# Transposing u with the DMA crossbar in an attention and mixer kernel, and splitting its last output chunk

## The chip, the core and the metric

The kernel runs on one core of a Trainium2 chip, as one launch. The metric is device time in microseconds (us), the median of several runs.

The core has a matrix engine (TensorE, PE in the profile; its weight loads are listed apart as PEld), a vector engine (VectorE, DVE), a scalar engine (ScalarE, ACT), GpSimd (POOL) and a sync engine (SyncE, SP) that here only issues DMAs. PE writes to PSUM; DVE and ACT move the results from there to SBUF, the on-chip memory from which PE reads.

## The reference

Blockwise causal attention over 8 batches, 8 heads, 576 positions and a head width of 64, and behind it one mixer layer with a token part and a channel part:

```python
# B, H, S, D = 8, 8, 576, 64; blocks of 64
scores = scale * np.matmul(q, k.transpose(0, 1, 3, 2))
scores = np.where(block_i >= block_j, scores, -1e9)
attn = softmax(scores)                      # with + 1e-09 in the denominator
x = (attn @ v).transpose(0, 2, 1, 3).reshape(B, S, 512)

xt = x.transpose(0, 2, 1)
h  = np.maximum(xt @ w_tok1, 0.0) @ w_tok2  # w_tok1 576 x 256, w_tok2 256 x 576
u  = x + h.transpose(0, 2, 1)
h2 = np.maximum(u @ w_ch1, 0.0) @ w_ch2     # w_ch1 512 x 1536, w_ch2 1536 x 512
out = u + h2                                # float32, 8 x 576 x 512
```

Inputs are float32; the kernel works in bfloat16 with float32 sums in PSUM.

## The kernel before

Each batch goes through these stages.

- **Attention** (scores at L415, exponentials on ACT at L444, product with v at L514, division on DVE at L535 and L541). It leaves x of the batch in `x_sb`, positions on the partitions, in five chunks of 128 positions (the last holds 64).
- **Token mix** (`token_mix`). Matmuls at L592 give `aT`; matmuls at L663 give h in the layout of x, and DVE adds x to it at L684. This leaves u in `u_sb`: four chunks of 128 positions by 512 channels. The last 64 positions of an even batch and of the odd batch behind it share one chunk, `um_sb`, one per pair of batches.
- **Transpose of u.** Channel-up needs u with the channels on the partitions. For batch 0 (`direct`), PE computes the transposed u by matmuls (L621, L636). For every later batch, PE transposes each 128×128 block of u against an identity matrix (L697), four blocks to one PSUM bank, and ACT or DVE copies the bank (L712, L714) to `uT`, or to `umT` for the shared chunk, which is transposed with the odd batch.
- **Channel-up** (`channel_up`): 12 column groups of 4 matmuls of 512 columns (L736), 48 matmuls a batch, then a ReLU on ACT or DVE to `gT` (L560, L562). The shared chunk does the same with 128 columns (`channel_up_mixed`, L763).
- **Channel-down** (`channel_down`): four chunks of 12 matmuls (L802), an add of u on DVE into `o_sb` (L818), and a store. Two chunks share one `o_sb` buffer and one store of 512 KB (L839). The shared chunk (`mixed=True`) has 12 matmuls, one add and two stores of 128 KB (L831), one to each batch of its pair. All stores go out on SP's queue.

Buffers come in rings: `uT` and `umT` have two, `u_sb`, `x_sb` and `o_sb` three, the PSUM pool `mm` four banks. `uT` of batch b is buffer b modulo 2, so it is free when the channel-up of batch b − 2 has read it. `o_sb` buffers are taken in turn by a counter, `out_n`, two for a batch and one for a shared chunk: the last store of batch 7 reads buffer 0, and the last shared chunk of all, the kernel's final work, gets buffer 1.

The order of instructions is not that of the program text. Every piece of work is an `Op` with engines it may run on, a cost, its dependences, a priority (lower goes first), and buffers that it takes and gives. `Plan.run` simulates the engines with these costs and lists the ops by planned start; the instructions are then issued in that order on each engine's queue, and each queue runs in order. Waits for real dependences are put in by the framework. A DMA has a cost on its issuing queue and a transfer time `xfer`, behind which its users become ready. Attention has priorities around −1000, token mix around −500, the channel stages from 0 up, so channel work fills the time that attention and token mix leave on PE. After attention ends, only channel work and the last token mixes are left.

L318 and L296 are the q and k loads and their transposes on DVE, L343 the v loads, all issued from POOL.

Of the kernel before, what the change touches and what calls it, by code (L numbers as in the profile page):

```python
# [11 lines left out]
BF16 = mybir.dt.bfloat16  # L12
# [3 lines left out]
ADD = mybir.AluOpType.add  # L16
# [113 lines left out]
def kernel(  # L130
# [26 lines left out]
    def ring(n, shape, dtype, name, pool=sb):  # L157
        return [pool.tile(shape, dtype, name=f"{name}{i}", uniquify=False) for i in range(n)]
# [10 lines left out]
    x_sb = ring(3, [128, 5, DM], BF16, "x_sb")  # L169
    u_sb = ring(3, [128, 4, DM], BF16, "u_sb")  # L170
    um_sb = ring(2, [128, DM], BF16, "um_sb")
    uT = ring(2, [128, NDM, 512], BF16, "uT")
    umT = ring(2, [128, NDM, 128], BF16, "umT")
    aT = ring(2, [128, NDT, DM], BF16, "aT")
    gT = ring(2, [128, NDC, 512], BF16, "gT")
# [25 lines left out]
    def bank_of(note):  # L201
        return mm[note["slot"]]
# [4 lines left out]
    def reads(key, op):  # L207
        readers.setdefault(key, []).append(op)
        return op

    def reuse(key):
        return readers.pop(key, [])

    def mm_cost(n, count):
        return count * max(n / 2400 + 0.003, 0.033)
# [4 lines left out]
    def dve_cost(n, speed=1):  # L220
        return 0.09 + n * 0.00104 / speed
# [343 lines left out]
    def token_mix(b, x_done, w1_ready, w2_ready):  # L565
# [14 lines left out]
        for half in range(NH):  # L580
            cols = slice(W * half, W * half + W)
            xs = x_done[8 // NH * half : 8 // NH * (half + 1)]
            p0 = prio + ((-494, -600)[half] if direct else 0)
            a_done = []
            for tts in ((0, 1),) if direct else ((0,), (1,)):
                bank = {}

                def emit(o, tts=tts, bank=bank, cols=cols):
                    for n, tt in enumerate(tts):
                        for c in range(5):  # L590
                            w = w1o_sb if c == 4 and odd else w1_sb[:, c]
                            nc.tensor.matmul(  # L592
                                out=bank_of(bank)[:, W * n : W * n + W],
                                lhsT=w[:, 128 * tt : 128 * (tt + 1)],
                                rhs=xt[:, c, cols],
                                start=(c == 0),
                                stop=(c == 4),
                            )

                op = P.add(  # L600
                    "PE", mm_cost(W, 5 * NH), emit, xs + w1_ready[odd] + a_war, p0,
                    take=[(BANK, bank)], urgent=direct and half == 1,
                )
                reads(("x", b % 3), op)

                def emit(o, tts=tts, bank=bank, cols=cols):
                    relu(
                        o,
                        at[:, tts[0] : tts[-1] + 1, cols],
                        bank_of(bank).rearrange("p (t d) -> p t d", d=W),  # L610
                    )

                a_done.append(P.add(EVAC, evac_cost(512), emit, [op], p0, give=[bank], urgent=direct and half == 1))
            a_all += a_done
            for m in range(NDM // NH * half, NDM // NH * (half + 1)) if direct else ():
                bank = {}

                def emit(o, m=m, bank=bank):
                    ps = bank_of(bank)
                    for c in range(4):  # L620
                        nc.tensor.matmul(  # L621
                            out=ps[:, 128 * c : 128 * c + 128],
                            lhsT=xt[:, c, 128 * m : 128 * (m + 1)],
                            rhs=ident,
                            start=(c == 0),
                            stop=False,
                        )

                first = P.add(
                    "PE", mm_cost(128, 4), emit, xs + pads["ident"] + uT_war, p0 + 1,  # L630
                    take=[(BANK, bank)], urgent=half == 1,
                )

                def emit(o, m=m, bank=bank):
                    for t in range(NDT):
                        nc.tensor.matmul(  # L636
                            out=bank_of(bank),
                            lhsT=at[:, t, 128 * m : 128 * (m + 1)],
                            rhs=w2_sb[:, t, 0:512],
                            start=False,  # L640
                            stop=(t == NDT - 1),
                        )

                op = P.add("PE", mm_cost(512, 2), emit, a_done + w2_ready + [first], p0 + 1, urgent=half == 1)
                reads(("a", b % 2), op)
                reads(("x", b % 3), op)

                def emit(o, m=m, bank=bank):
                    if o.engine == "ACT":
                        nc.scalar.copy(uT[b % 2][:, m, :], bank_of(bank))  # L650
                    else:
                        nc.vector.tensor_copy(uT[b % 2][:, m, :], bank_of(bank))

                done.append(P.add(EVAC, evac_cost(512), emit, [op], p0, give=[bank], urgent=direct and half == 1))
        if direct:
# [31 lines left out]
            reads(("x", b % 3), op)  # L687
            u_done.append(op)

        for si in range(4 * direct, 4 + odd):  # L690
            bank = {}

            def emit(o, si=si, bank=bank):
                ps = bank_of(bank).bitcast(BF16)[:, 0:512]
                src = ut[:, si, :] if si < 4 else umt
                for m in range(NDM):
                    nc.tensor.transpose(  # L697
                        ps[:, 128 * m : 128 * (m + 1)], src[:, 128 * m : 128 * (m + 1)], ident
                    )

            deps = [u_done[si]] + pads["ident"]
            deps += uT_war if si < 4 else reuse(("umT", pair % 2)) + um_first[pair]
            op = P.add(
                "PE", mm_cost(128, 4), emit, deps, prio + 2 + 0.1 * si, take=[(BANK, bank)]
            )
            reads(("u", b % 3) if si < 4 else ("um", pair % 2), op)

            def emit(o, si=si, bank=bank):
                ps = bank_of(bank).bitcast(BF16)[:, 0:512].rearrange("p (m s) -> p m s", m=NDM)
                dst = uT[b % 2][:, :, 128 * si : 128 * si + 128] if si < 4 else umT[pair % 2]  # L710
                if o.engine == "ACT":
                    nc.scalar.copy(dst, ps)  # L712
                else:
                    nc.vector.tensor_copy(dst, ps)  # L714

            op = P.add(
                EVAC, {"ACT": act_cost(512), "DVE": dve_cost(512, 2)}, emit, [op], prio, give=[bank]
            )
            (done if si < 4 else um_done).append(op)
# [8 lines left out]
    def channel_up(b, uT_done, wc1_ready, prio):  # L728
        g_war = reuse(("g", b % 2))
        done = []  # L730
        for cc in range(NDC):
            bank = {}

            def emit(o, cc=cc, bank=bank):
                for m in range(NDM):
                    nc.tensor.matmul(  # L736
                        out=bank_of(bank),
                        lhsT=wc1_sb[:, m, 128 * cc : 128 * (cc + 1)],
                        rhs=uT[b % 2][:, m, :],
                        start=(m == 0),  # L740
                        stop=(m == NDM - 1),
                    )

            op = P.add("PE", mm_cost(512, 4), emit, uT_done + wc1_ready[cc] + g_war, prio + 0.1 * cc, take=[(BANK, bank)])
            reads(("uT", b % 2), op)

            def emit(o, cc=cc, bank=bank):
                relu(o, gT[b % 2][:, cc, :], bank_of(bank))

            done.append(P.add(EVAC, evac_cost(512), emit, [op], prio, give=[bank]))  # L750
        return done
# [31 lines left out]

    out_n = [0]

    def channel_down(b, g_done, wc2_ready, u_done, prio, mixed=False):
        chunks = [None] if mixed else list(range(4))
        gt = gmT[b // 2 % 2] if mixed else gT[b % 2]
        ut = um_sb[b // 2 % 2] if mixed else u_sb[b % 3]
        for n, si in enumerate(chunks):  # L790
            bank = {}
            prev = None
# [6 lines left out]
            for part in range(3):  # L799
                def emit(o, part=part, c0=c0, bank=bank):  # L800
                    for cc in range(4 * part, 4 * part + 4):
                        nc.tensor.matmul(  # L802
                            out=bank_of(bank),
                            lhsT=gt[:, cc, c0 : c0 + 128],
                            rhs=wc2_sb[:, cc, :],
                            start=(cc == 0),
                            stop=(cc == NDC - 1),
                        )
# [98 lines left out]
```

## Time and profile before

| | |
|---|---|
| median of 3 runs | 330.89 us (330.43 to 331.6) |
| the profiled execution: its time | 328.57 us |
| the profiled execution: its span, first to last instruction | 326.8 us |
| mean granted PE clock | 0.977 |
| busy PE, DVE, ACT, POOL | 95%, 50%, 51%, 19% of the span |
| DMA, mean | 89 GB/s |

A row of the profile names the line of the kernel, the engine, the operation, what it writes and reads, shapes, a count (x), the busy time in us and the mean length of one in ns, and, behind the bar, how long the engine sat idle just before and what released it. A matmul's length is a latency in a pipeline, so matmuls overlap. A row of a table by stretches gives start and end, the length, then for each engine the busy time and the number of instructions, then the granted clock (1.00 is full), the DMA engines' share and GB/s. A row of the timeline gives start, length, engine, line and work.

### The profile page before, as it was taken

Reading aid. Unit: us, or ns where it says so; the run is one execution under the profiler, and the core shown is the slowest. Engines: PE = TensorE matmul, PEld = TensorE weight load, DVE = VectorE, ACT = ScalarE, POOL = GpSimd, SP = SyncE. Lnnn points to the kernel's source line nnn. Section 1 sums busy time; section 2 is a strip of 40 time slices with the busy share of each in tenths; the row PEclk is TensorE's granted clock in tenths of the full one; section 3 lists DMA queues with packets and bytes.
Section 4 is the critical chain, followed back from the end, with each engine's and each line's share of the span. In section 5 each row is a group of like instructions: output and inputs, shape, how many; then the busy total and the mean of one; then the engine's idle time right before and its main releaser. Section 6 shows DMA issues by size and latency. Waiting matters only on the chain.

```text
span 326.8 us, 7206 instructions
## 1 busy us (share of the span) xinstructions
PE 309.6 (95%) x3031; PEld 161.0 (49%) x3074; DVE 164.8 (50%) x383; ACT 167.6 (51%) x231; POOL 61.3 (19%) x97
## 2 busy tenths in 40 slices
PE   6799997999999999999999999999999999999994
PEld 2256454354556455454555456544544654444641
DVE  6637946696779498496574556035114112011012
ACT  4854873548769636648756766402702711613600
POOL 8657532411421502500500000000000000000000
PEclk9659999999999999999999999999999999999999
DMA  8999999957893907940901100013011002103013
GB/s 220 209 208 190 199 193 124 156 120 118 126 149 58 129 4 143 185 55 2 69 6 66 66 2 2 0 64 98 0 61 70 0 20 111 33 2 128 2 64 96
DMA packets 46800, 29.01 MB, mean 89 GB/s; under 512 B 34064, under 2 KB 37520, under 8 KB 46768
## 3 DMA queue, kind: packets, MB, share of 16 engines
q0 software_dynamic: 41200, 17.93, 44.9%
q1 hardware_dynamic: 5280, 10.03, 8.8%
q10 hardware_dynamic: 288, 0.59, 0.5%
q8 instruction: 24, 0.39, 0.5%
q14 instruction: 8, 0.07, 0.1%
HBM read 35.85 MB, written 9.44 MB: 139 GB/s over the span
## 4 chain that ended last, share of the span: by engine, by line
PE 85%; DVE 7%; ACT 3%; issue 2%; DMA 2%; ACTq 0%
PE mm L802 28%; PE mm L736 26%; PE sc L415 9%; PE mm L514 7%; PE mm L592 6%; PE mm L663 4%; PE mm L763 3%; DVE x_sb L541 2%; ACT e_sb L444 2%; DMA gT<-in_q_dram 2%; PE mm L697 1%; DVE u_sb L684 1%; DVE qT L318 1%; DVE rinv L535 1%; PE mm L636 1%
## 5 line engine op out<-in xcount | busy, mean ns | idle before, releaser
L444 ACT ACTIVATE e_sb<-sc 128x1024 bf16<-128x1024 f32 x96 | 93.2, 1021 | 49.0 <-PE sc L415 48.3
L736 PE MATMUL mm<-uT,wc_sb 128*128 128x512 bf16 x371 | 87.9, 379 | 1.1 <-issue 0.3
L802 PE MATMUL mm<-wc_sb,gT 128*128 128x512 bf16 x367 | 85.8, 379 | 1.3 <-issue 0.5
L560 ACT ACTIVATE gT<-mm 128x512 bf16<-128x512 f32 x73 | 43.5, 598 | 71.9 <-PE mm L736 71.6
L736 PEld LDWEIGHTS <-wc_sb 128*128 128x128 bf16 x384 | 36.2, 98 | 45.8 <-issue 4.5
L818 DVE TENSOR_TENSOR o_sb<-mm,u_sb 128x512 f32<-128x512 f32 x32 | 22.1, 691 | 70.9 <-PE mm L802 70.8
L802 PEld LDWEIGHTS <-gT 128*128 128x128 bf16 x384 | 36.1, 98 | 43.8 <-issue 3.9
L415 PE MATMUL sc<-qT,kT 32*128 32x64 bf16 (+4 forms) x768 | 39.2, 290 | 4.2 <-ACT e_sb L444 2.3
L343 POOL DMA_DIRECT2D v<-in_v_dram x35 | 29.6, 858 | 42.9 <-PE sc L415 21.0
L514 PEld LDWEIGHTS <-e_sb 128*128 128x128 bf16 x896 | 32.3, 99 | 10.1 <-issue 3.5
L514 PE MATMUL mm<-v,e_sb 128*128 128x65 bf16 x896 | 34.4, 196 | 2.0 <-DVE e_sb L486 1.9
L541 DVE TENSOR_TENSOR x_sb<-mm,rinv 128x320 bf16<-128x320 f32 x64 | 30.7, 488 | 1.6
L684 DVE TENSOR_TENSOR u_sb<-mm,x_sb 128x512 bf16<-128x512 f32 x32 | 20.9, 683 | 12.0 <-PE mm L663 11.8
L415 PEld LDWEIGHTS <-kT 32*128 32x128 bf16 x768 | 13.6, 95 | 25.1 <-issue 20.1
L562 DVE TENSOR_SCALAR gT<-mm 128x512 bf16<-128x512 f32 x23 | 15.8, 687 | 16.2 <-PE mm L736 16.1
L318 DVE STREAM_TRANSPOSE kT<-kraw 128x576 int32<-128x576 int32 (+1 forms) x20 | 20.1, 1029 | 1.6 <-PE sc L415 1.5
L318 DVE STREAM_TRANSPOSE qT<-qraw 128x576 int32<-128x576 int32 (+1 forms) x20 | 20.0, 1022 | 0.2
L663 PE MATMUL mm<-aT,w_sb 128*128 128x512 bf16 x72 | 19.7, 380 | 0.4 <-issue 0.2
L592 PE MATMUL mm<-x_sb,w_sb 128*128 128x512 bf16 (+1 forms) x81 | 18.1, 360 | 0.5 <-DVE x_sb L541 0.4
L486 DVE MEMSET e_sb<- 64x128 uint32 (+1 forms) x72 | 10.5, 153 | 15.3 <-ACT e_sb L444 12.2
L535 DVE RECIPROCAL rinv<-mm 128x5 f32<-128x5 f32 x64 | 11.2, 183 | 8.4 <-PE mm L514 8.1
L296 POOL DMA_DIRECT2D kraw<-in_k_dram x15 | 8.4, 559 | 27.9 <-DVE kT L318 13.9
(59 smaller groups left out, 188.2 us busy)
## 6 DMA issues: line engine op xcount, KB each, us to landing
out_dram<-o_sb SPq DMA_DIRECT2D x16, 512.0 KB, 2.8
kraw<-in_k_dram POOLq DMA_DIRECT2D x15, 288.0 KB, 5.7
qraw<-in_q_dram POOLq DMA_DIRECT2D x15, 288.0 KB, 6.5
v<-in_v_dram POOLq DMA_DIRECT2D x28, 128.0 KB, 5.7
wc_sb<-in_moe_w_ch_dram POOLq DMA_DIRECT2D x8, 192.0 KB, 8.4
wc_sb<-in_moe_w_ch_dram POOLq DMA_DIRECT2D x3, 512.0 KB, 10.1
gT<-in_v_dram POOLq DMA_DIRECT2D x4, 256.0 KB, 8.5
out_dram<-o_sb SPq DMA_DIRECT2D x8, 128.0 KB, 2.4
```

Source lines behind the costliest of these rows:

```text
L318: nc.vector.transpose(dst[:, 0:S, :] .rearrange("p s e -> p (s e)") .bitcast(I32) .rearrange("p (a k) -> p k a", k=NB)[:, k0:k1], raw2.bit ...
L343: nc.gpsimd.dma_start(out=dst, in_=src)
L415: nc.tensor.matmul(out=sc[h // 2][:, h % 2, c0 : c0 + w], lhsT=kT[i][r, j0 : j0 + 128, par], rhs=qT[i][r, i0 : i0 + w, par], start=(par == 0),
L444: nc.scalar.activation(dst, sc[h0 // 2][:, :, 0:n], EXP, scale=scale)
L514: nc.tensor.matmul(out=u[:, I, 0:65], lhsT=w, rhs=vt[:, J, head, 0:65], start=(J == 0), stop=(J == I),)
L541: nc.vector.tensor_tensor(out=xt[:, :, 64 * head : 64 * head + 64], in0=u[:, :, 0:64], in1=ri.to_broadcast([128, 5, 64]), op=MULT,)
L560: nc.scalar.activation(dst, src, RELU)
L592: nc.tensor.matmul(out=bank_of(bank)[:, W * n : W * n + W], lhsT=w[:, 128 * tt : 128 * (tt + 1)], rhs=xt[:, c, cols], start=(c == 0), stop ...
L663: nc.tensor.matmul(out=bank_of(bank), lhsT=w2_sb[:, t, c0 : c0 + 128], rhs=at[:, t, :], start=(t == 0), stop=(t == NDT - 1),)
L684: nc.vector.tensor_tensor(out=dst, in0=bank_of(bank)[r, :], in1=xt[r, si, :], op=ADD)
L736: nc.tensor.matmul(out=bank_of(bank), lhsT=wc1_sb[:, m, 128 * cc : 128 * (cc + 1)], rhs=uT[b % 2][:, m, :], start=(m == 0), stop=(m == NDM ...
L802: nc.tensor.matmul(out=bank_of(bank), lhsT=gt[:, cc, c0 : c0 + 128], rhs=wc2_sb[:, cc, :], start=(cc == 0), stop=(cc == NDC - 1),)
```

## The change

From batch 2 on, u is transposed by DMAs on SP's queue (`dma_start_transpose`) in place of PE's transposes and their copies. A batch has two of them, each for two chunks of 128 positions (128 × 1024 elements, 256 KB), with planned costs of 2.0 us on SP and 3.0 us of transfer; an odd batch has one more for the shared chunk (128 × 512, 128 KB). Batch 0 stays as it was, and batch 1 still transposes on PE, its shared chunk with it. `uT` is laid out as four position chunks of four channel groups of 128, in place of four channel groups of 512 positions, so channel-up's moving operand is now four runs of 128 columns.

The last shared chunk of the kernel is computed by `last_down`: two halves of 256 columns, each with 12 matmuls, an add of its own, and two stores of 64 KB, one issued from SP and one from ACT. The halves use `o_sb[0]` and `o_sb[1]`, and the plan lets a half's matmuls begin when the last store from its buffer is done.

```diff
-    uT = ring(2, [128, NDM, 512], BF16, "uT")
+    uT = ring(2, [128, 4, NDM, 128], BF16, "uT")
...
+                    ps = bank_of(bank).rearrange("p (c s) -> p c s", c=4)
                     if o.engine == "ACT":
-                        nc.scalar.copy(uT[b % 2][:, m, :], bank_of(bank))
+                        nc.scalar.copy(uT[b % 2][:, :, m, :], ps)
                     else:
-                        nc.vector.tensor_copy(uT[b % 2][:, m, :], bank_of(bank))
+                        nc.vector.tensor_copy(uT[b % 2][:, :, m, :], ps)
...
-        for si in range(4 * direct, 4 + odd):
+
+        crossbar = b >= 2
+        for f in range(2 if crossbar else 0):
+            def emit(o, f=f):
+                nc.sync.dma_start_transpose(
+                    out=uT[b % 2][:, 2 * f : 2 * f + 2].rearrange("p c m s -> p (c m) s"),
+                    in_=ut[:, 2 * f : 2 * f + 2, :].rearrange("p c d -> p (c d)"),
+                )
+
+            op = P.add("SP", 2.0, emit, u_done[2 * f : 2 * f + 2] + uT_war, prio, xfer=3.0)
+            reads(("u", b % 3), op)
+            done.append(op)
+        if crossbar and odd:
+            def emit(o):
+                nc.sync.dma_start_transpose(out=umT[pair % 2], in_=umt)
+
+            op = P.add("SP", 1.0, emit, [u_done[4]] + reuse(("umT", pair % 2)) + um_first[pair], prio, xfer=1.0)
+            reads(("um", pair % 2), op)
+            um_done.append(op)
+        for si in () if crossbar else range(4 * direct, 4 + odd):
...
-                dst = uT[b % 2][:, :, 128 * si : 128 * si + 128] if si < 4 else umT[pair % 2]
+                dst = uT[b % 2][:, si] if si < 4 else umT[pair % 2]
...
-                        rhs=uT[b % 2][:, m, :],
+                        rhs=uT[b % 2][:, :, m, :],
...
+    def last_down(gt, ut, deps, prio):
+        for f in range(2):
+            cols = slice(256 * f, 256 * f + 256)
+            bank = {}
+
+            def emit(o, cols=cols, bank=bank):
+                for cc in range(NDC):
+                    nc.tensor.matmul(
+                        out=bank_of(bank)[:, 0:256],
+                        lhsT=gt[:, cc, :],
+                        rhs=wc2_sb[:, cc, cols],
+                        start=(cc == 0),
+                        stop=(cc == NDC - 1),
+                    )
+
+            op = P.add("PE", mm_cost(256, NDC), emit, deps + reuse(("o", f)), prio + 0.1 * f, take=[(BANK, bank)])
+
+            def emit(o, f=f, cols=cols, bank=bank):
+                nc.vector.tensor_tensor(
+                    out=o_sb[f][:, 0, 0:256], in0=bank_of(bank)[:, 0:256], in1=ut[:, cols], op=ADD
+                )
+
+            op = P.add("DVE", dve_cost(256), emit, [op], prio, give=[bank])
+            for kk in range(2):
+                def emit(o, f=f, kk=kk, cols=cols):
+                    queue = nc.sync if o.engine == "SP" else nc.scalar
+                    queue.dma_start(
+                        out=out[B - 2 + kk, 512:576, cols],
+                        in_=o_sb[f][64 * kk : 64 * kk + 64, 0, 0:256],
+                    )
+
+                P.add(("SP", "ACT")[kk], 0.5, emit, [op], prio, xfer=4 * 0.06)
+
     def channel_down(b, g_done, wc2_ready, u_done, prio, mixed=False):
...
+        if mixed and b == B - 1:
+            return last_down(gt, ut, g_done + wc2_ready + u_done, prio)
```

## The prediction

> **What bounds the kernel now.** I read the page's busy times and slices first, then the chain that ended last, then busy time by stage.
>
> ```profile
> span 326.8 us, 7206 instructions
> PE 309.6 (95%) x3031; PEld 161.0 (49%) x3074; DVE 164.8 (50%) x383; ACT 167.6 (51%) x231; POOL 61.3 (19%) x97
> PEclk9659999999999999999999999999999999999999
> PE 85%; DVE 7%; ACT 3%; issue 2%; DMA 2%; ACTq 0%
> ```
>
> TensorE (PE) is busy 95% of the span, at the full granted clock after the first few slices, and carries 85% of the chain that ended last. Less PE work should shorten the span nearly one for one. The average hides stages, so I cut the span: attention with channel work as filler (57 to 209 us), then channel work alone (209 to 306).
>
> ```profile
> 57.00:134.00 77.00, 74.79 (x961) 40.11 (x974) 59.87 (x131) 50.15 (x64) 22.44 (x34) 1.00 0.86 114
> 134.00:209.00 75.00, 73.17 (x911) 39.99 (x922) 44.30 (x108) 48.64 (x67) 6.30 (x8) 1.00 0.33 42
> 209.00:306.00 97.00, 96.38 (x502) 46.42 (x511) 21.00 (x33) 32.31 (x55) 0.00 (x0) 1.00 0.14 49
> ```
>
> The columns are the stretch, then busy PE, weight loads, DVE, ACT, POOL, clock, DMA share, GB/s. PE idles 77 − 74.79 = 2.2, 75 − 73.17 = 1.8 and 0.6 us. It ends every stage last; DVE at 59.87 of 77 us is the only near rival, and only in the first.
>
> **What is removed: 108 transposes on PE.** The trace has 128 at L697 (112 of u_sb, 16 of um_sb). Batch 1 keeps 20; batches 2 to 7 lose 6 × 16 + 3 × 4 = 108. With them go their 27 copies out of PSUM.
>
> ```profile
> L697 PE MATMUL mm<-ident,u_sb 128*128 128x128 bf16 x112 | 9.1, 219 | 1.2 <-DVE um_sb L684 0.5 <-DVE x_sb L541 0.2
> L697 PE MATMUL mm<-ident,um_sb 128*128 128x128 bf16 x16 | 1.5, 218 | 0.1
> L712 ACT COPY uT<-mm 128x512 bf16<-128x512 bf16 x12 | 6.9, 595 | 1.5 <-PE mm L697 1.4
> L714 DVE COPY uT<-mm 128x512 bf16<-128x512 bf16 x16 | 6.2, 416 | 14.7 <-PE mm L697 14.5
> ```
>
> The 219 ns of one is a pipelined latency, not its price. The price is the time from the first transpose of a group to the start of PE's next work, read in the timeline of PE (start, length, work), one group per fence here:
>
> ```profile
> 98.14 1.13 PE L697 MATMUL mm<-ident,u_sb 128*128 128x128 bf16 x12
> 99.47 0.38 PE L697 MATMUL mm<-ident,u_sb 128*128 128x128 bf16 x4 [0.21 <-DVE um_sb L684]
> 99.80 0.59 PE L736 MATMUL mm<-uT,wc_sb 128*128 128x512 bf16 x2
> ```
> ```profile
> 235.69 1.29 PE L697 MATMUL mm<-ident,u_sb 128*128 128x128 bf16 x16
> 236.82 1.46 PE L802 MATMUL mm<-wc_sb,gT 128*128 128x512 bf16 x6
> ```
> ```profile
> 259.29 1.23 PE L697 MATMUL mm<-ident,u_sb 128*128 128x128 bf16 x16
> 260.36 1.95 PE L763 MATMUL mm<-umT,wc_sb 128*128 128x128 bf16 x32
> ```
>
> Late groups cost 236.82 − 235.69 = 1.13 and 260.36 − 259.29 = 1.07 us for 16, so 0.069 us each. The group at 98 us cost 99.80 − 98.14 = 1.66, since it waited for u to be added on DVE. Lower end: 108 × 0.069 = 7.4 us. Upper end: busy time of L697 alone over the seven stretches (each a group or two) that hold the 108, first and last stretch and the sum:
>
> ```profile
> 97.00:100.00 3.00, 1.39 (x16) 0.97 (x16) 1.00 0.33 57
> ...
> 259.00:260.60 1.60, 1.22 (x16) 0.97 (x16) 1.00 0.00 0
> sum 16.10, PE 8.67 PEld 6.80; mean PE 1.24 PEld 0.97
> ```
>
> 8.67 us counts each group's pipeline tail, which overlaps the next work, but leaves out its waits. I take 7.4: the waits for DVE stood in the attention stage, where PE may meet another wait in their place. The 27 copies (0.416 us on DVE, 0.595 on ACT) I cost at nothing: neither engine ends a stage. Where ACT and DVE are full, their absence helps a little.
>
> **What is added: 15 crossbar DMAs on SP's queue**, two of 256 KB for each of batches 2 to 7, one of 128 KB for each of batches 3, 5 and 7. Before, uT was ready a copy after the transposes; now after a DMA. What hides this is distance. uT has two buffers, so batch b's transpose can start when its u is added and the channel-up of batch b − 2 is done. The stretches below are cut at the channel-ups (busy time of L736 alone; the second bracket, weight loads, has x48 for a whole batch):
>
> ```profile
> 102.00:143.50 41.50, 0.36 (x2) 0.01 (x1) 1.00 0.87 107
> 143.50:161.60 18.10, 10.82 (x46) 4.28 (x48) 1.00 0.32 30
> 161.60:185.80 24.20, 0.30 (x2) 0.00 (x0) 1.00 0.31 57
> 185.80:200.30 14.50, 10.52 (x45) 4.37 (x48) 1.00 0.00 1
> 200.30:219.70 19.40, 0.42 (x2) 0.00 (x0) 1.00 0.07 28
> 219.70:234.60 14.90, 10.57 (x46) 4.66 (x48) 1.00 0.18 54
> 234.60:258.20 23.60, 10.66 (x49) 4.70 (x48) 1.00 0.12 45
> 258.20:273.10 14.90, 0.36 (x2) 0.00 (x0) 1.00 0.10 36
> 273.10:285.25 12.15, 10.42 (x47) 4.68 (x49) 1.00 0.22 65
> ```
>
> Batches 2 to 6 run their up in the stretches with x48 (x49 for the last), and batch 7 from 285.25. Batch 2's u is complete by 99.47, so 143.5 − 99.5 = 44 us. For the others I count from the buffer's release: batch 4 from 161.6 to 219.7, 58; batch 5 from 200.3 to 234.6, 34; batch 6 from 234.6 to 273.1, 38; batch 7 from 258.2 to 285.25, 27 us. The least is 27 for two DMAs in one queue: 13.5 us each.
>
> No row shows a crossbar transpose. Nearest rows, with KB each and us from issue to landing, and the software queue:
>
> ```profile
> out_dram<-o_sb SPq DMA_DIRECT2D x16, 512.0 KB, 2.8
> kraw<-in_k_dram POOLq DMA_DIRECT2D x15, 288.0 KB, 5.7
> out_dram<-o_sb SPq DMA_DIRECT2D x8, 128.0 KB, 2.4
> q0 software_dynamic: 41200, 17.93, 44.9%
> ```
>
> Lower end 2.4 us. Upper end from that queue's packets: 0.449 × 16 × 326.8 us / 41,200 = 57 ns of one engine for a packet. As 256-byte runs, 256 KB is 1,024 packets, so 57 ns × 1,024 / 16 = 3.6 us over 16 engines, about 6 with the 2.4 us. As 32-byte runs it is 29 us, beyond the cover. I take 6, which is nearest the 288 KB load's 5.7. Two cost 12 us, under 27: hidden, zero on the path. SP's queue is in order: a transpose behind a store whose data is late would wait with it, and a store behind a transpose would too. The planner orders SP by planned time, and stores fall inside channel-downs, after the release points above; I cost this at zero.
>
> The Trainium skill, "VectorE: DVE Perf Modes", The three transpose paths, speaks against the change: 390 ns for 128×128 on TensorE against 1309 ns through the crossbar, with the advice to use TensorE where PSUM will do. An estimate from that page: 8 blocks in series are 10.5 us, 21 for a batch, still under the 27, so by it the sum stands, but with only 6 us to spare. The trace's 0.069 us in a group already differs from its 390 ns; no run yet shows the 1309.
>
> **Layout.** uT becomes four 128-column pieces, so channel-up streams four runs. Its price if each run cost a separate 128-column matmul: 16 at 258.40 to 259.29 are 0.0556 each, four 0.2225, against 7.99 / 37 = 0.216 for 512 columns.
>
> ```profile
> 258.40 1.06 PE L763 MATMUL mm<-umT,wc_sb 128*128 128x128 bf16 x16
> 297.71 7.99 PE mm L736 x37
> ```
>
> So 0 to 384 × 0.0065 = 2.5 us; I take 0, since the instruction count and columns are the same. Copies into four runs exist before (L712, 595 ns) and cost no surcharge I can see.
>
> **The tail.** Before, the last chunk's add is followed by two stores from o_sb[1]: the buffers are taken in turn, modulo three. The new function names o_sb[0] and o_sb[1]; o_sb[0] is what batch 7's last store is still reading.
>
> ```profile
> 322.01 0.69 DVE L818 TENSOR_TENSOR o_sb<-mm,um_sb 128x512 f32<-128x512 f32 x1 [1.84 <-PE mm L802]
> ```
> ```profile
> 320.20 0.37 SPq L839 DMA_DIRECT2D out_dram<-o_sb  x1
> 322.73 1.11 SPq L831 DMA_DIRECT2D out_dram<-o_sb  x2
> ```
>
> Before: the second store starts at about 323.3 and lands 2.4 later, 325.7. After, in the same clock: the half in o_sb[0] must wait for the store issued at 320.20 to land, 320.20 + 2.8 = 323.0. Its add is some 0.4 us (an estimate, a little over half of 0.69), its stores go out at 323.4 on two queues and land at 325.8 or so: +0.1. The other half, planned first since its buffer is free, is done by then. Without that wait the add would start at 322.0 and all would end near 324.9, −0.8. Upper end +0.6, a second issue (1.11 / 2) in series. I take +0.1.
>
> **Sum.** −7.4 + 0 + 0 + 0.1 = −7.3. The profiled execution took 328.57 us around its span of 326.8, so 321.3 for it; the median of the runs shown is 330.89, so 323.6.
>
> **The rivals.**
> *The attention stage gives nothing back.* If ACT or DVE is what PE really follows there, only the transposes after 209 us count: 4 + 16 + 16 = 36, 36 × 0.069 = 2.5 us, so 328.4. For it: DVE's 59.87 of 77 us, and the wait at 99.47. Against it: PE idles only 2.2 and 1.8 us there, and channel work can always be drawn forward. 0.14.
>
> *The transposes are late (slower).* If one 256 KB DMA takes over 13.5 us, batch 7's channel-up waits for it. At 20 us: batch 7 stalls 40 − 27 = 13, batch 6 40 − 38 = 2, batch 5 (with its 128 KB) 50 − 34 = 16: 31 us, less 7.3, so some 355. The stalls of batches 7 and 5 together are 4.5 × D − 61, so the sign turns at D = 15 us. For it: no row shows such a DMA, and 32-byte runs would mean 29 us. Against it: 2.8 us for 512 KB. 0.09.
>
> *A new order eats it.* Every instruction after batch 2 is replanned. Doubling PE's 4.0 us of idle in 57 to 209, with the 2.5 us of the layout, leaves about 330.0. Nothing in the profile speaks for it. 0.09, of which 0.04 slower.
>
> **How the numbers follow.** My forecast has 0.68, its own range 321.4 (−8.67 and −0.8) to 326.2 (the layout's 2.5 us lost). Up to the attention rival gives 329.0; down, 321.0. What is left out, late transposes and a lost gain, is under 0.2. About 0.3%, 1.0 us, is what this measurement can tell from no change: faster 0.82, within 0.05, slower 0.13.
>
> **What the next profile would show.** Right: L697 with 20 matmuls, PE busy down by some 7 us, the 15 transposes at SP landing within about 6 us, no PE wait on a DMA before L736, L736 still at 0.216 us a matmul, and the first of the two last adds released by PE, the second by a DMA. Wrong: PE idle before L736 with a DMA as releaser, landings over 13 us, 4-run matmuls spaced wider, or PE idle in 57 to 209 above 4 us.

## The result, and the profile after

The changed kernel took 321.09 us (median; 319.41 to 321.27), against 331.25 us for the kernel before on the same chip. The ratio is 0.9685, with a 95% interval of 0.9646 to 0.9724: some 9 to 12 us faster. The forecast was 323.6 us, a gain of 7.3, in a range of 321.0 to 329.0. Scaled to the 330.89 of the forecast, the ratio makes 320.5, below the range. The direction held, and PE is what bounds the kernel, as forecast. The gain was some 3 us larger: about 2 us of that are in the work itself, about 1 in how runs of this kernel scatter (below).

The page of the changed kernel, its opening and the chain by engine:

```profile
span 319.2 us, 7057 instructions
PE 306.0 (96%) x2978; PEld 156.4 (49%) x2978; DVE 159.7 (50%) x370; ACT 160.7 (50%) x218; POOL 61.3 (19%) x97
PE 90%; ACT 3%; DMA 3%; DVE 2%; issue 1%; ACTq 0%; DVEq 0%
```

PE still bounds it, more clearly than before: 90% of the chain against 85%, and DVE's share fell from 7% to 2%. Weight loads fell from 3074 to 2978: 108 transposes gone, 12 matmuls more in the split tail. The same stretches as before show where PE idles now (0.5, 0.2 and 0 us):

```profile
57.00:134.00 77.00, 76.49 (x958) 39.46 (x956) 59.38 (x129) 48.31 (x61) 23.88 (x36) 1.00 1.02 135
134.00:209.00 75.00, 74.81 (x901) 38.77 (x900) 43.48 (x107) 46.22 (x61) 6.55 (x8) 1.00 0.43 52
209.00:306.00 97.00, 97.00 (x522) 46.93 (x521) 18.33 (x28) 32.24 (x54) 0.00 (x0) 1.00 0.24 62
```

These idle times mislead a little: the trace of before has 371 of 384 matmuls of L736, that of after all 384, and a missing record reads as idle. Start times of weight loads don't have that fault (x384 for L736), so from here I compare one stretch of equal work: from the middle of the first channel-down (its 25th matmul) to the start of the last channel-down. Cutting the executions there gives these rows, first of before, then of after (columns as in the tables by stretches):

```profile
68.15:308.83 240.68, 236.49 (x2329) 124.43 (x2362) 116.89 (x258) 126.33 (x180) 24.86 (x35) 1.00 0.37 61
```
```profile
69.85:300.88 231.03, 230.76 (x2256) 117.19 (x2254) 111.30 (x244) 119.44 (x167) 24.85 (x35) 1.00 0.51 79
```

The same work takes 9.65 us less at a clock of 1.00 in both. What lies ahead of it takes 69.85 − 68.15 = 1.7 us more in this execution of the changed kernel, which is clock (below), and the tail behind it 18.3 − 18.0 = 0.3 us more; both take away from the 9.65. A stretch cut like this repeats closely: 231.03 in a second profile of the same kernel, where the runs scatter over 2 us and more. It is the measure of the experiments.

The crossbar DMAs, from the rows of L695 (uT), and the tail on DVE:

```profile
L695 SPq DMA_TRANSPOSE uT<-u_sb x12: 1233/1254/1962, 97.1 to 253.1; - x12
DMA to landing us min/median/max: 3.3/4.5/5.9
```
```profile
311.54 0.69 DVE L873 TENSOR_TENSOR o_sb<-mm,u_sb 128x512 f32<-128x512 f32 x1 [0.17 <-PE mm L857]
312.80 0.42 DVE L824 TENSOR_TENSOR o_sb<-mm,um_sb 128x256 f32<-128x256 f32 x1 [0.56 <-PE mm L813]
315.25 0.42 DVE L824 TENSOR_TENSOR o_sb<-mm,um_sb 128x256 f32<-128x256 f32 x1 [2.04 <-DMA out_dram<-o_sb]
```

A 256 KB transpose lands 4.5 us after its issue, and no matmul waits for one. The second of the two last adds waits 2.04 us for the DMA that still reads o_sb[0].

### The profile page after: what moved, and what is told of

Read it like the earlier page. It is cut to its first block, busy times and chain, and to the rows that moved or that the text cites. A ratio compares the mean times of both kernels' runs of the same rounds, so it can differ in the third digit from the quotient of the medians.

```text
span 319.2 us, 7057 instructions
## 1 busy us (share of the span) xinstructions
PE 306.0 (96%) x2978; PEld 156.4 (49%) x2978; DVE 159.7 (50%) x370; ACT 160.7 (50%) x218; POOL 61.3 (19%) x97
## 3 DMA queue, kind: packets, MB, share of 16 engines
q1 hardware_dynamic: 19584, 13.44, 18.2%
## 4 chain that ended last, share of the span: by engine, by line
PE 90%; ACT 3%; DMA 3%; DVE 2%; issue 1%; ACTq 0%; DVEq 0%
PE mm L857 28%; PE mm L756 27%; PE sc L415 10%; PE mm L514 10%; PE mm L592 6%; PE mm L664 6%; PE mm L783 3%; ACT e_sb L444 2%; DMA gT<-in_q_dram 2%; DMA out_dram<-o_sb 1%; DVE qT L318 1%; PE mm L636 1%; DVE x_sb L541 0%; DVE o_sb L873 0%; DVE gT L562 0%
## 5 line engine op out<-in xcount | busy, mean ns | idle before, releaser
L857 PE MATMUL mm<-wc_sb,gT 128*128 128x512 bf16 x384 | 88.2, 379 | 0.0
L560 ACT ACTIVATE gT<-mm 128x512 bf16<-128x512 f32 x75 | 44.7, 598 | 69.8 <-PE mm L756 69.6
L514 PEld LDWEIGHTS <-e_sb 128*128 128x128 bf16 x896 | 33.4, 101 | 10.6 <-issue 4.1
L514 PE MATMUL mm<-v,e_sb 128*128 128x65 bf16 x896 | 35.4, 199 | 1.9 <-DVE e_sb L486 1.9
L541 DVE TENSOR_TENSOR x_sb<-mm,rinv 128x320 bf16<-128x320 f32 x64 | 30.9, 489 | 1.6
L562 DVE TENSOR_SCALAR gT<-mm 128x512 bf16<-128x512 f32 x21 | 14.4, 688 | 14.1 <-PE mm L756 14.1
L664 PE MATMUL mm<-aT,w_sb 128*128 128x512 bf16 x80 | 20.9, 380 | 0.0
L486 DVE MEMSET e_sb<- 64x128 uint32 (+1 forms) x72 | 10.5, 153 | 13.6 <-ACT e_sb L444 10.2
```

Source lines behind the costliest of these rows:

```text
L514: nc.tensor.matmul(out=u[:, I, 0:65], lhsT=w, rhs=vt[:, J, head, 0:65], start=(J == 0), stop=(J == I),)
L541: nc.vector.tensor_tensor(out=xt[:, :, 64 * head : 64 * head + 64], in0=u[:, :, 0:64], in1=ri.to_broadcast([128, 5, 64]), op=MULT,)
L560: nc.scalar.activation(dst, src, RELU)
L664: nc.tensor.matmul(out=bank_of(bank), lhsT=w2_sb[:, t, c0 : c0 + 128], rhs=at[:, t, :], start=(t == 0), stop=(t == NDT - 1),)
L857: nc.tensor.matmul(out=bank_of(bank), lhsT=gt[:, cc, c0 : c0 + 128], rhs=wc2_sb[:, cc, :], start=(cc == 0), stop=(cc == NDC - 1),)
```

## The experiments

Theories: **A**, the removed transposes were worth more than 7.4 us; **B**, the sum was right and the rest of the difference is the scatter of runs. When A held, it split: PE's waits for u, the copies, or a new order. "Stretch" is the one defined above.

**The changed kernel again.** No edit.

> The changed kernel again, beside the kernel before, so that each run's span and clock can be set side by side. Theory A (the removed transposes were worth more than priced: their whole stretches on PE, some 9 us, waits included): the ratio stays near 0.969, and the profile's stretch between the first channel-down and the last one is some 9.6 us shorter than before, 254.2 to about 244.6. Theory B (the sum of 7.3 was right and the rest of the measured 10 us is the clock: the profile shown of before missed a clock dip near 53 us that its other runs have): runs of before spread over 2 to 3 us with their granted clock, 0.977 for the short ones and 0.973 for the long ones, and runs of equal clock differ by 7.3 us only. Both can hold in part.

319.5 us, ratio 0.9693 (0.9647 to 0.9739). Both hold in part. The runs of before fall on steps with their granted clock: 328.8 us at 0.977, 330.2 to 331.1 at 0.970 to 0.971, 331.5 to 331.8 at 0.966 to 0.967. The changed kernel has 319.2 to 319.6 at 0.975 and longer ones at less. The forecast was drawn from an execution on the shortest step (328.57 at 0.977); like against like, 328.57 and 319.43 (this run's profiled execution), the gain is 9.1 us, not 7.3. So A carries the 2 us, and the uneven mix of steps the last one of the medians' 10.

**Crossbar without the split tail, and split tail without crossbar.**

```diff
-        if mixed and b == B - 1:
-            return last_down(gt, ut, g_done + wc2_ready + u_done, prio)
```

> The changed kernel with its last chunk computed and stored whole, as before: the crossbar and the layout alone. If the split tail costs 0.1 to 0.35 us, as its wait for the store of o_sb[0] suggests (add released by a DMA, 2.0 us of wait in the changed kernel's profile), this is 0.1 to 0.35 us faster than the changed kernel. Rival: the split gains the 0.8 us of an unhindered half, and this is some 0.8 us slower than the changed kernel.

> The kernel before with the split last chunk alone. Same question from the other side: between +0.35 and 0 us against before if the wait for o_sb[0] eats the split's gain, -0.8 us if it does not. In the profile one of the two 256-column adds is released by a DMA.

Crossbar alone: 321.35 us, ratio 0.9718 (0.9679 to 0.9757), stretch 231.03, tail 18.5. Split tail alone: 331.29, ratio 0.9996 (0.9969 to 1.0024), tail 18.2; its second add too was released by the out_dram DMA, after 2.05 us. All of the gain is the crossbar's. The split is worth nothing within 0.3 us; the tails of like kernels differ by 0.4 (18.3 and 18.7 of the same code), so its sign can't be told. The rival's −0.8 didn't come.

**Halves in free buffers.** The changed kernel with:

```diff
-    deps + reuse(("o", f))
+    deps + reuse(("o", f + 1))
...
-    out=o_sb[f][:, 0, 0:256]
+    out=o_sb[f + 1][:, 0, 0:256]
...
-    in_=o_sb[f][64 * kk : 64 * kk + 64, 0, 0:256]
+    in_=o_sb[f + 1][64 * kk : 64 * kk + 64, 0, 0:256]
```

> The changed kernel with the two halves in o_sb[1] and o_sb[2], whose stores are done or nearly done by then, in place of o_sb[0] and o_sb[1]. If the wait for the buffer is what ate the split's gain, the second add starts 0.1 us after its matmuls, some 1 us earlier than now, and the kernel is 0.8 to 1.1 us faster than the changed one. Rival (the stores themselves are the tail's bound, issue and landing in series): no change.

320.02 us, ratio 0.9676 (0.9642 to 0.971). The tail is 17.1 us against 18.3, and the second add is released by PE:

```profile
312.86 0.42 DVE L824 TENSOR_TENSOR o_sb<-mm,um_sb 128x256 f32<-128x256 f32 x1 [0.56 <-PE mm L813]
314.17 0.42 DVE L824 TENSOR_TENSOR o_sb<-mm,um_sb 128x256 f32<-128x256 f32 x1 [0.89 <-PE mm L813]
```

The buffer choice ate 1.2 us of the split. In medians the step is inside the scatter.

**The layout alone.** The changed kernel without the split tail and with all transposes back on PE; only `uT` in four pieces is left of the change.

```diff
-        crossbar = b >= 2
+        crossbar = b >= 99
```

> The kernel before with the new layout of uT alone (four runs of 128 columns for channel-up), transposes still on PE, last chunk whole. The prediction took 0 with an upper end of 2.5 us: 0 if the four runs stream as one, +2.5 us (channel-up matmuls spaced 0.2225 in place of 0.216 us) at the upper end. A gain would mean that the copies into the contiguous pieces are faster.

Ratio 0.9973 (0.9952 to 0.9995), and a stretch of 240.72 against 240.68: four runs of 128 columns cost nothing.

**The transposes back on PE, without the crossbar's being undone.** The changed kernel plus 27 groups of four transposes, of zeros. They have the old cost and priority but need no `uT` buffer, and the planner places them anew:

```diff
+            op = P.add(
+                "PE", mm_cost(128, 4), emit, [u_mm[si]] + pads["ident"] + pads["zeros"], prio + 2 + 0.1 * si,
+                take=[(BANK, bank)], give=[bank],
+            )
```

and the same of u, with `u_done[si]` as its dependence. Neither has copies.

> The changed kernel with 108 transposes put back on PE at the places of the old ones, but of a tile of zeros that is ready from the start, into a bank that nobody copies out. It gives back the slots on PE without the wait for u and without the copies. If only the slots count (108 x 0.069), it is 7.4 us slower than the changed kernel. If what was under-priced is the wait of PE for the DVE adds of u, some 2 to 2.5 us of the gain stay.

> As the run with zeros, but the 108 transposes read u, and so wait for the DVE add of their chunk, as they did before; still no copies. If PE's wait for u is the part that was under-priced, this is about 9 us slower than the changed kernel, 1.5 to 2 us slower than the run with zeros. If the 27 copies on ACT and DVE were the part, it is 7.4 us slower, as the run with zeros.

328.99 us (ratio 0.9923, 0.9901 to 0.9945) and 329.26 (0.9942, 0.9916 to 0.9969). The stretches, zeros first:

```profile
70.58:308.80 238.22, 235.28 (x2338) 124.08 (x2362) 107.35 (x238) 123.24 (x173) 24.91 (x35) 1.00 0.47 77
```
```profile
70.37:308.21 237.84, 234.77 (x2336) 123.88 (x2362) 108.03 (x239) 122.55 (x172) 24.86 (x35) 1.00 0.47 77
```

Against 231.03 that is +7.2 and +6.8 us. Placed as they are here, the transposes cost about what the slots were priced at, 7.4, and those of u no more than those of zeros. Some 2.5 to 2.8 us of the 9.65 are still missing. It doesn't follow that PE's wait for u cost nothing in the kernel before, because the order there was another; the orders are compared below.

**The copies back.** First beside the transposes of u, into a spare tile; then alone, from a ready tile in SBUF, so that no PSUM bank is held.

```diff
+            def emit(o, si=si, bank=bank):
+                ps = bank_of(bank).bitcast(BF16)[:, 0:512]
+                cast(o, spare[0 if o.engine == "ACT" else 1], ps)
+
+            P.add(EVAC, {"ACT": act_cost(512), "DVE": dve_cost(512, 2)}, emit, [op], prio, give=[bank])
```

> As the run whose 108 transposes on PE read u, with the 27 copies put back as well, on ACT or DVE as the planner has it, into a spare tile that nobody reads. Only the feeding of channel-up by the crossbar is left of the change. That run's stretch from the first to the last channel-down was 251.7 us, before it was 254.2, after 244.5. Theory C (the copies are the term priced wrong: costed at nothing, worth some 2 us): the stretch is 254 us or nearly so. Theory D (the copies are free as the prediction had it, and the 2 us are the luck of a new order): it stays near 251.7, within 0.7 us.

> The changed kernel with 27 copies of the old size alone on ACT or DVE, from a ready tile in SBUF (float32) into a spare tile, each behind the add of its chunk of u; no transposes on PE. If the copies cost by the time that they take from ACT and DVE, the stretch from the first to the last channel-down grows from 244.5 by 1.5 to 2.5 us. If they cost only by holding a PSUM bank and PE's hand-over, or not at all, it grows by less than 0.7 us.

With transposes and copies 332.48 us (ratio 1.0046, 1.0025 to 1.0066), copies alone 321.89 (0.9718, 0.9686 to 0.975):

```profile
71.20:312.22 241.02, 239.06 (x2364) 124.13 (x2362) 114.50 (x255) 128.27 (x183) 24.85 (x35) 1.00 0.46 76
```
```profile
71.50:302.55 231.05, 230.79 (x2256) 117.26 (x2254) 115.54 (x253) 128.90 (x185) 24.85 (x35) 1.00 0.51 79
```

Together all of the gain is gone (241.02 against 240.68 before). Alone they cost nothing (231.05), though DVE and ACT do 4.2 and 9.5 us more work in the stretch. So the copies' time is free, and yet 3.2 us come back with them: a wait on the chip, or the order that the planner makes.

**The same order with copies cut short, or not issued.** Both are planned exactly as the kernel with copies; one copies two columns of 512, the other issues no copy.

```diff
-                ps = bank_of(bank).bitcast(BF16)[:, 0:512]
-                cast(o, spare[0 if o.engine == "ACT" else 1], ps)
+                ps = bank_of(bank).bitcast(BF16)[:, 0:2]                     # the first
+                cast(o, spare[0 if o.engine == "ACT" else 1][:, 0:2], ps)    # the first
+                pass                                                         # the second
```

> As the run with transposes of u and copies put back on PE, in exactly its order, but each of the 27 copies takes two columns in place of 512: the hand-over from PE and the bank's release stay, the copy's length goes. The stretch up to the last channel-down was some 2.5 us longer with copies than without. If the banks' being held for the length of a copy is what costs, most of the 2.5 us goes, to within 0.7 us of the run without copies. If it is the order that the planner makes with copies in it, or the hand-over, the stretch stays as with full copies.

> The same order again, with the copies planned but none issued. If it stays as with full copies, the cost is the order alone: the planner, counting a copy as a load on ACT and DVE and a bank as held until it is done, places PE's work worse. If it falls to the run without copies, the cost is on the chip: the copies in the queues of ACT and DVE, or the banks that they hold.

331.85 us (ratio 1.0038, 0.9994 to 1.0082) and 331.34 (0.9982, 0.9946 to 1.0017). The stretches, two columns first:

```profile
68.15:308.41 240.26, 238.44 (x2364) 124.00 (x2362) 110.90 (x255) 122.95 (x183) 24.86 (x35) 1.00 0.45 76
```
```profile
70.21:310.48 240.27, 238.43 (x2363) 123.97 (x2361) 109.31 (x241) 121.44 (x170) 24.86 (x35) 1.00 0.46 76
```

With no copy issued the stretch is still 240.27, 2.4 us over the kernel that has the same instructions in another order (237.84). So 2.4 us are the order, and the copies themselves, here beside transposes, 241.02 − 240.27 = 0.75.

Most of the 2.4 us can be found in the traces. Priced as the prediction priced three groups, from the first transpose of a group to the start of PE's next work, the 108 transposes take 6.64 us in the order without copies and 8.60 us in the order with them, 1.96 more. In the second order PE reaches transposes before their u is added. These are the rows of idle time before the transposes and what ended it, with the times (a wait can stand in them twice, at the weight load and at the matmul), first of the run without copies, then of the run with copies planned only:

```profile
  DVE u_sb L686: 0.2, 1
```
```profile
  DVE u_sb L687: 1.1, 4
  DVE um_sb L687: 0.2, 1
```

One place as an example, in the same order of runs. Without copies the planner puts the second half behind some channel-up work; with them, PE stands and waits for u:

```profile
251.01 0.65 PE L701 MATMUL mm<-ident,u_sb 128*128 128x128 bf16 x8
251.50 1.03 PE L773 MATMUL mm<-uT,wc_sb 128*128 128x512 bf16 x4
252.36 0.61 PE L701 MATMUL mm<-ident,u_sb 128*128 128x128 bf16 x8
252.81 1.46 PE L773 MATMUL mm<-uT,wc_sb 128*128 128x512 bf16 x6
```
```profile
252.94 0.65 PE L702 MATMUL mm<-ident,u_sb 128*128 128x128 bf16 x8
253.79 0.40 PE L702 MATMUL mm<-ident,u_sb 128*128 128x128 bf16 x4 [0.20 <-DVE u_sb L687]
254.03 1.03 PE L779 MATMUL mm<-uT,wc_sb 128*128 128x512 bf16 x4
```

The kernel before has an order of this kind. Three of its eight groups stand in the prediction; these are the other five:

```profile
119.04 1.52 PE L697 MATMUL mm<-ident,u_sb 128*128 128x128 bf16 x16
120.51 0.38 PE L697 MATMUL mm<-ident,um_sb 128*128 128x128 bf16 x4
120.84 1.02 PE L802 MATMUL mm<-wc_sb,gT 128*128 128x512 bf16 x3
```
```profile
162.16 0.90 PE L697 MATMUL mm<-ident,u_sb 128*128 128x128 bf16 x12
162.99 0.31 PE L415 MATMUL sc<-qT,kT 32*128 32x64 bf16 x16
163.40 0.38 PE L697 MATMUL mm<-ident,u_sb 128*128 128x128 bf16 x4
163.62 0.39 PE L697 MATMUL mm<-ident,um_sb 128*128 128x128 bf16 x4
164.14 0.81 PE L802 MATMUL mm<-wc_sb,gT 128*128 128x512 bf16 x2
```
```profile
203.26 0.63 PE L697 MATMUL mm<-ident,u_sb 128*128 128x128 bf16 x8
204.13 0.61 PE L697 MATMUL mm<-ident,u_sb 128*128 128x128 bf16 x8 [0.24 <-DVE x_sb L541]
204.76 1.02 PE L592 MATMUL mm<-x_sb,w_sb 128*128 128x512 bf16 x3
```
```profile
228.56 0.39 PE L697 MATMUL mm<-ident,um_sb 128*128 128x128 bf16 x4
228.78 1.03 PE L736 MATMUL mm<-uT,wc_sb 128*128 128x512 bf16 x4
```

With the three of the prediction the eight groups make 1.66 + 1.80 + 0.83 + 0.74 + 1.50 + 0.22 + 1.13 + 1.07 = 8.95 us. That is most of the 9.65 that went with them. The waits inside are of two kinds. At 99.47 PE waits for the add of u. At 204.13 it was released by the division at L541, which reads a PSUM bank; that PE waited there for a free bank is inferred. Why the planner places the transposes so when copies are planned, and the last 0.7 us of the 9.65, were not traced.

**Late transposes.** Each crossbar DMA issued twice, then four times, with the plan unchanged.

```diff
+                for _ in range(2):      # or 4
                     nc.sync.dma_start_transpose(...)
```

> Every crossbar transpose of the changed kernel is issued twice, the second over the first, with the plan's costs unchanged. Two of 256 KB in a row make 9 to 10 us of one, under the 13.5 us where the prediction said that the cover ends: no change, within 0.5 us. If the transposes were nearly late already, PE waits on a DMA before the channel-ups of batches 5 and 7.

> Every crossbar transpose four times. If each waits for the one before, 256 KB take some 18 us, over the 13.5 us: batch 7 stalls by 2 x 18 - 26 = 10 us, batch 5 by about as much, and the kernel is 10 to 25 us slower than the changed one. If the four run into each other at 1.25 us of issue each, 256 KB take 8 us and nothing changes. The landings of the pieces show which.

Twice: 320.48 us, ratio 0.9708 (0.9656 to 0.976), stretch 231.03, no change. Four times: 343.71 us, ratio 1.0378 (1.0323 to 1.0433). The waits of PE there, and the landings of its 48 pieces:

```profile
PE mm L758 <- DMA uT<-u_sb: 16.6, 3, 9.1
```
```profile
DMA to landing us min/median/max: 3.0/3.2/7.9
```

Each piece waits for the one before, which writes the same tile, so 256 KB take about 4 × 3.2 = 13 us, and the stretch grows by 23.9 us, a part of which is the clock (0.96 in it, where the others have 1.00). SP's queue shows batch 6's eight pieces, its stores and batch 7's eight:

```profile
249.22 22.80 SPq L696 DMA_TRANSPOSE uT<-u_sb  x8
272.07 1.10 SPq L896 DMA_DIRECT2D out_dram<-o_sb  x2
273.27 22.74 SPq L696 DMA_TRANSPOSE uT<-u_sb  x8
```

The cover is real, but it ends sooner than forecast (13.5 us a DMA for batch 7, 15 for the sign to turn): at 13 us the kernel is already slower than before. The forecast counted batch 7's 27 us from the release of its buffer. Here its transposes start only behind those of batch 6, which fill SP's queue up to 272 us, and PE waits 9.1 us for them. The order on SP's queue, which the sum put at zero, ends the cover here.

**Batch 1 through the crossbar too**, with the free buffers.

```diff
-        crossbar = b >= 2
+        crossbar = b >= 1
```

> The changed kernel with the halves in o_sb[1] and o_sb[2], and batch 1 through the crossbar too: 20 more transposes off PE. By the price of whole stretches (2.0 us for batch 1's group in the profile of before) 2 us faster than the run with free buffers, 1.4 us by 0.069 each. The cover is thin: its u is added at 68 us, channel-up starts at 79 us in the changed kernel, and a pair of 256 KB transposes lands within some 6 us. If the cover fails, PE waits on a DMA before the channel-up of batch 1 and the gain shrinks or turns.

319.23 us, ratio 0.9632 (0.9612 to 0.9652), the lowest of all versions, though its interval still touches that of the free buffers alone (0.9642 to 0.971). From the start of the first channel-down to that of the last it is 243.35 us against 244.54 with free buffers alone, 1.2 us, less than the 1.4 to 2.0 expected; PE waits for no crossbar DMA.

**PE's hole near 51 us filled** with eight matmuls on zeros, with the free buffers.

```diff
+        P.add("PE", 8 * 0.216, emit, pads["zeros"], 1e6, take=[(BANK, bank)], give=[bank], at=47.25)
```

> The changed kernel with free buffers and eight matmuls on zeros placed in PE's idle 1.9 us near 51 us. If the clock dip near 53 us (granted 0.50 for some 3 us in the changed kernel's profile, absent in that of before) follows from that hole, no run of this kernel shows it: clock 0.975 and up in all runs, and the median is 1.3 us below that of the free-buffer kernel, whose runs fall on both sides. If the dip has another cause, no change, or +0.2 us where the matmuls are in the way.

320.18 us, ratio 0.9686 (0.9652 to 0.972). Below are the clock rows of the changed kernel, where PE idles from 51.5 to 53.4, and then of this run.

```profile
52.00:53.00 1.00, 0.00 (x0) 0.00 (x0) 0.00 (x0) 1.00 (x2) 0.00 (x0) 0.94 1.04 207
54.00:55.00 1.00, 1.00 (x23) 1.00 (x21) 0.69 (x3) 0.00 (x0) 0.00 (x0) 0.50 0.17 32
```
```profile
52.00:53.00 1.00, 1.00 (x6) 0.48 (x5) 0.00 (x0) 1.00 (x2) 0.00 (x0) 1.00 1.16 223
54.00:55.00 1.00, 0.88 (x28) 0.88 (x29) 0.52 (x4) 0.00 (x0) 0.00 (x0) 1.00 0.14 23
```

The dip is gone from the profile, and four of six runs have a clock of 0.979, higher than any run of the other kernels. That fits a dip that comes from the hole, though not every time. Two runs still have 0.970 and 0.971; the profiled one is one of them, and its low clock lies earlier (0.50 from 10 to 25 us, where the changed kernel has 0.69 from 10 to 15 and 0.50 behind it). But it didn't pay: the order of instructions behind the eight matmuls is another, and the stretch between the channel-downs grew from 244.54 to 245.86 us at a clock of 1.00, by about the size of the dip.

## Why the prediction was wrong, point by point

- **What bounds.** Right: PE, in all stages. The rival by which the attention stage gives nothing back fell: the three groups after 209 us make 2.4 of the 8.95 us, and the stretch lost 9.65.
- **The 108 slots, 7.4 us.** This is the step that failed. The sum took the spacing in late groups, 0.069 us, for all 108, and put the waits of the earlier groups at nothing: "PE may meet another wait in their place". It met next to none: PE's idle time between 57 and 209 us is 0.7 us in the changed kernel. The eight groups had taken 8.95 us, waits included, and the stretch lost 9.65. The upper end of 8.67 us was busy time without the waits, so it was too low as well. Transposes that meet few waits do cost what the sum says, 7.2 us with zeros and 6.8 with u; in the order with copies they cost 240.27 − 231.03 = 9.2.
- **The 27 copies, costed at nothing.** Right for their time on ACT and DVE (231.05 against 231.03 alone, 0.75 us beside the transposes). What the sum left out is that a copy is also an op in the plan that holds a bank, and that with it the planner places the transposes where they wait: 2.4 us. The forecast named a new order only as a loss, "Nothing in the profile speaks for it", and gave the gain side no room in the range. Transposes of u, the order and the copies together make 6.8 + 2.4 + 0.75 = 10.0 us, measured as 241.02 − 231.03; the change itself took off 9.65.
- **Hidden transposes, zero on the path.** Right, with 4.5 us in place of the 6 taken. The Trainium skill's 1309 ns a block ("VectorE: DVE Perf Modes", The three transpose paths) gives, as an estimate, 10.5 us for these eight blocks; the trace shows 4.5. Its advice to use TensorE did not suit this kernel, where the latency was covered and PE's time was not.
- **The layout at 0.** Right, 0.04 us.
- **The tail, +0.1.** Right in mechanism: one add behind PE, one behind the DMA that read o_sb[0]. Its size, +0.1, lies within the scatter of the tails, so it is not confirmed.
- **The range's lower edge, 321.0.** The bounds of the slots and the tail make 321.4; for the 0.4 us below that the prediction gives no sum. Waits of the slots on top of their busy time, and a baseline whose runs have three steps of clock, would have moved the edge to 318 or 319.

## What to carry to other kernels

Where one engine is busy 95% of the time, price work removed from it by the time from its start to the start of the next work, not by its length, and do so for every group: waits inside a group go with it. Where a planner orders everything, taking ops out of the plan changes the order of the rest, here by 2.4 us: put that in the range on both sides, and test it by planning an op without issuing it. To see effects of a microsecond in runs that scatter by two or three, cut a stretch of equal work out of the profile, between two starts that every version has, where the clock is full.

## What was not expected of the hardware

The kernel's scatter goes with the granted clock of PE: runs of before lie at 328.7, about 330.6 and about 331.5 us, for a mean clock of 0.977, 0.970 and 0.966. One of the dips follows an idle of PE of 1.9 us, drops the clock to 0.50 for some 3 us (53 to 56 us in the profile of the changed kernel), and doesn't come in every execution: the profiles of before and of the changed kernel's second run have the same hole and no dip. The issue of a 256 KB crossbar transpose keeps SP's queue for 1.25 us, and one issued when the one before has landed lands 3.2 us after its issue.
